# Regrouped early transposes, a split last K tile and a later store of a small vector in a diffusion-transformer block

## The chip, the cores and the metric

The kernel runs on one core of one Trainium2 chip. The metric is device time in microseconds (us) of one execution. A ratio between two kernels is taken over the fast runs of one job, with its 95% interval; it is not quite the ratio of the medians quoted beside it. The jobs ran on different chips, so times are compared within a job.

TensorE multiplies matrices, VectorE (DVE) and ScalarE (ACT) work elementwise, GpSimd (POOL) helps, and SyncE (SP) issues most DMA transfers. In profile lines "PE" is TensorE, "pk", "pacc", "pm", "pn", "pt" are accumulator tiles, and times count from the first instruction. A transfer is issued when it is handed to the DMA queues and lands when its data has arrived. "The chain" is the work that ended last, followed back through what each step waited for.

## The reference

Two batches of 256 tokens, width D = 1152, which is nine chunks of 128. Token tiles 0, 1 belong to batch 0 and tiles 2, 3 to batch 1.

```python
mod = (silu(c) @ w_mod)          # six vectors: shift_a, scale_a, gate_a, shift_m, scale_m, gate_m
h   = layernorm(x) * (1 + scale_a) + shift_a
q, k, v = split(h @ wqkv)
a   = attention(q, k, v) @ wo
x   = x + gate_a * a
h2  = layernorm(x) * (1 + scale_m) + shift_m
out = x + gate_m * (gelu(h2 @ w_fc1) @ w_fc2)
```

## The kernel before

At the start everything is scarce: x and the weights arrive by DMA, the normalised x (`xn`) is transposed on TensorE chunk by chunk, scaled by `1 + scale_a`, and at once used for K. The `w_scale_a` weights come in four groups; `scale_group(3)` serves chunks 6, 7, 8. I call the landing of that last group "the gate".

```python
KGROUPS = [(0, 2), (2, 4), (4, 6), (6, 9)]     # chunks served by each w_scale_a group
KM1 = 6                                        # K tiles 0..5 run chunk by chunk, 6..8 later as panels

def k_step(k, c0=0, c1=T):                     # chunk k into six K tiles, token columns c0:c1
    for m in range(KM1):
        ...
        nc.tensor.matmul(pk[m][:, c0:c1], w_k[:, k, m*P:(m+1)*P], hT0[:, k, c0:c1], ...)

    # ... cut: tiles 0 to 2, chunks 0 and 1
    recip1(3)
    norm1(3, 0, CUT, "d")
    k_step(0, N, N + P)
    k_step(1, N, N + P)
    pt_3 = transpose_x([2, 3], [0, 1])
    for i, k in enumerate((2, 3)):
        modulate(pt_3, i, k, 0, 0, N, "a")     # "a": on ScalarE, "d": on VectorE
    pt_4 = transpose_x([0, 1], [3])
    ...
    k_step(2, 0, N)
    k_step(3, 0, N)
    # ... cut
    nc.vector.transpose(s_rows[...], sT[...])  # s = silu(c), as rows
    store_by_quadrant(s_dram[...], s_rows, B)  # read back at about 28 us as s_b
    # ... cut
    k_step(4)
    scale_group(3)("d")                        # the gate
    modulated_transpose(6)
    k_step(5)
    modulated_transpose(7)
    k_step(6)
    modulated_transpose(8)
    k_step(7)
    k_step(8)
    # ... cut: evictions of K tiles 0..5, panels 6 and 7
    shift_a = vec_section(sT, w_shift_a, "shift_a")   # the shift section, 36 narrow matmuls
    k_panel(8)
    # then hT = hT0 + shift_a, and Q's matmuls
```

## Time and profile before

| | |
|---|---|
| time, median of 3 runs | 243.78 us (243.46 to 243.98) |
| span of the profiled run | 242.1 us, clock 0.999 |
| gate: last `w_scale_a` group issued, landed | 11.13, 20.16 us |
| shift section starts | 30.73 us |
| Q's first matmul | 33.95 us |

These are lines of the page: busy us and share of the span of each engine, then busy tenths in 40 slices of the span.

```profile
PE 235.7 (97%) x1689; PEld 142.8 (59%) x1698; DVE 93.2 (38%) x207; ACT 70.3 (29%) x140; POOL 31.9 (13%) x48
...
PE   8899999999999999999999999999999999999994
```

TensorE is nearly always busy, so only its waits count. The Trainium skill, "Perfetto Trace Analysis", section on the tensor engine instruction, says that the end of a matmul in the profile is an estimate. The trace fits that: a matmul over 512 columns is drawn 379 ns long, but the next one starts 216 ns after it. I therefore measure a wait as start to start, less the usual spacing.

The chain that ended last, of the kernel before, around the gate (columns: start us, us, what, count):

```profile
11.13 9.03 DMA w_scale_a<-in_w_mod_dram
20.16 0.05 issue
20.21 0.83 PE pm L246 x27
21.04 0.24 PE pt L264 x4
21.28 1.29 PE pk L286 x6
```

The chain passes through the DMA. The last matmul in front of the gate started at 19.51, so the wait is 20.21 - 19.51 - 0.216 = 0.48 us.

The same view of the same kernel around the shift section (L417) and the start of Q (L495):

```profile
28.85 1.94 PE pk L315 x9
30.80 1.27 PE pn L417 x36
32.06 0.32 PE pk L315
...
34.11 1.94 PE pacc L495 x9
```

The nine matmuls of K's last tile (the record of one is missing) follow the section (from 32.00 to 33.95) and hide VectorE's preparation of Q's input.

Two more lines of the kernel before, from the timeline of ScalarE (the scalings for fc1) and from that of TensorE (the first fc1 matmuls, L786). The columns are start us, us, engine, line, operation, tiles and shapes, count.

```profile
94.53 3.06 ACT L671 ACTIVATE hT<-hT,shift_m,scale_m 128x256 bf16<-128x256 bf16 x6 [3.42 <-DMA hT<-xn]
...
97.68 1.07 ACT L671 ACTIVATE hT<-hT,shift_m,scale_m 128x256 bf16<-128x256 bf16 x2
```

### The profile page before, as it was taken

To read this page: it belongs to the slowest core of one execution; us is meant where nothing else is said; L and a number is where in the kernel's file an instruction comes from. 1 tells how busy PE (TensorE), PEld (TensorE's weight loads), DVE (VectorE), ACT (ScalarE), POOL (GpSimd) and SP (SyncE) were. 2 spreads that over 40 slices of the span, in tenths; PEclk is the share of its full clock that TensorE was granted. 3 is DMA by queue.
4 is the path that set the end of the run, shared out by engine and by line. 5 is a ranking of instruction groups with operands and counts; after the bars stand their busy time and mean duration, and the time that the engine had idled before them with its cause. 6 is when DMAs were issued, how large, how long until landed. Compare 5 with 4: busy or idle time off the path is not lost.

```text
span 242.1 us, 4022 instructions
## 1 busy us (share of the span) xinstructions
PE 235.7 (97%) x1689; PEld 142.8 (59%) x1698; DVE 93.2 (38%) x207; ACT 70.3 (29%) x140; POOL 31.9 (13%) x48
## 2 busy tenths in 40 slices
PE   8899999999999999999999999999999999999994
PEld 2585444466666666888844444444566656665673
DVE  3761550574694676720000039998010000000001
ACT  6542250543635174782222233322000000000000
POOL 1021000000310516300000000000233111111111
PEclk9999999999999999999999999999999999999999
DMA  6999999999999998799999999994971000000000
GB/s 223 325 331 342 383 357 225 328 376 274 251 323 357 385 278 218 201 226 328 328 328 258 218 298 329 326 327 120 311 224 33 19 16 16 20 20 27 21 16 16
DMA packets 76989, 54.48 MB, mean 225 GB/s; under 512 B 26011, under 2 KB 72491, under 8 KB 76971
## 3 DMA queue, kind: packets, MB, share of 16 engines
q1 hardware_dynamic: 76240, 53.02, 76.9%
q0 software_dynamic: 704, 1.20, 1.5%
q8 instruction: 13, 0.21, 0.4%
q14 instruction: 5, 0.04, 0.0%
q10 hardware_dynamic: 27, 0.00, 0.0%
HBM read 46.90 MB, written 1.19 MB: 199 GB/s over the span
## 4 chain that ended last, share of the span: by engine, by line
PE 90%; SPq 4%; DMA 4%; issue 0%; DVE 0%; DVEq 0%
PE pacc L850 29%; PE pacc L786 29%; PE pacc L689 7%; PE pacc L568 7%; PE pacc L495 5%; DMA w_scale_a<-in_w_mod_dram 4%; SPq L109 3%; PE pk L315 2%; PE pacc L503 2%; PE pk L286 2%; PE pa L603 1%; PE ps_s L523 1%; PE pn L417 1%; SPq L104 1%; PE pg L451 1%
## 5 line engine op out<-in xcount | busy, mean ns | idle before, releaser
L786 PE MATMUL pacc<-hT,w_f 128*128 128x256 bf16 (+1 forms) x427 | 70.3, 325 | 0.3
L850 PE MATMUL pacc<-w_f,gT 128*128 128x384 bf16 (+2 forms) x468 | 70.5, 314 | 0.0
L850 PEld LDWEIGHTS <-gT 128*128 128x128 bf16 x468 | 44.4, 98 | 26.2
L786 PEld LDWEIGHTS <-w_f 128*128 128x128 bf16 x432 | 42.2, 98 | 27.8 <-issue 0.2
L469 DVE SCALAR_TENSOR_TENSOR late<-w_gate_mT,late 128x1152 bf16<-128x1152 bf16 x18 | 24.4, 1358 | 35.8 <-DMA w_gate_mT<-in_w_mod_dram 35.2
L856 DVE TENSOR_TENSOR tmp<-pacc,gate 128x384 f32<-128x384 f32 (+2 forms) x13 | 6.8, 526 | 63.5 <-PE pacc L850 63.5
L824 ACT ACTIVATE gT<-pacc 128x512 bf16<-128x512 f32 x24 | 14.3, 597 | 32.3 <-PE pacc L786 32.3
L469 DVE SCALAR_TENSOR_TENSOR s_spill<-w_scale_m,s_b 128x1152 bf16<-128x1152 bf16 x12 | 16.3, 1357 | 8.9 <-DMA w_scale_m<-in_w_mod_dram 8.5
L858 POOL TENSOR_TENSOR o_sb<-tmp,x 128x384 bf16<-128x384 f32 (+1 forms) x12 | 11.6, 972 | 48.7 <-DVE tmp L856 48.7
L689 PE MATMUL pacc<-w_o,big 128*128 128x384 bf16 (+2 forms) x117 | 17.9, 314 | 0.0
L568 PE MATMUL pacc<-w_v,hT 128*128 128x384 bf16 x108 | 17.9, 326 | 0.0
L689 PEld LDWEIGHTS <-big 128*128 128x128 bf16 x117 | 11.0, 98 | 6.8 <-ACT big L611 0.2
L568 PEld LDWEIGHTS <-hT 128*128 128x128 bf16 x108 | 10.4, 98 | 7.0 <-issue 0.2
L286 PE MATMUL pk<-big,w_k 128*128 128x128 bf16 (+2 forms) x100 | 13.3, 276 | 0.2
L695 POOL TENSOR_TENSOR x<-tmp,x_sb 128x384 f32<-128x384 f32 (+1 forms) x11 | 9.8, 888 | 17.1 <-DVE tmp L694 9.4
L495 PE MATMUL pacc<-hT,w_q 128*128 128x512 bf16 x53 | 11.8, 379 | 0.1
L324 POOL DMA_DIRECT2D gates_dram<-grow x4 | 2.1, 522 | 69.8 <-DVE grow L810 69.8
L802 ACT ACTIVATE gT<-pacc 128x512 bf16<-128x512 f32 x12 | 6.9, 597 | 10.4 <-PE pacc L786 10.4
L286 PEld LDWEIGHTS <-w_k 128*128 128x128 bf16 x102 | 7.8, 97 | 3.1 <-issue 0.3
L495 PEld LDWEIGHTS <-w_q 128*128 128x128 bf16 x54 | 5.3, 98 | 6.4
L694 DVE TENSOR_TENSOR tmp<-pacc,gate 128x384 f32<-128x384 f32 (+2 forms) x13 | 6.7, 522 | 5.4 <-PE pacc L689 5.2
L169 PE MATMUL pwarm<-zeros 128*128 128x512 bf16 x21 | 7.4, 503 | 1.2 <-DVE eps_t L92 1.2
(99 smaller groups left out, 159.5 us busy)
## 6 DMA issues: line engine op xcount, KB each, us to landing
w_f<-in_w_fc_dram SPq DMA_DIRECT2D x14, 864.0 KB, 10.9
w_f<-in_w_fc_dram SPq DMA_DIRECT2D x2, 2592.0 KB, 10.2
w_f<-in_w_fc_dram SPq DMA_DIRECT2D x2, 1728.0 KB, 13.3
w_shift_a<-in_w_mod_dram SPq DMA_DIRECT2D x3, 864.0 KB, 11.2
w_v<-in_wqkv_dram SPq DMA_DIRECT2D x3, 864.0 KB, 6.0
w_gate_a<-in_w_mod_dram SPq DMA_DIRECT2D x3, 864.0 KB, 9.2
w_o<-in_wo_dram SPq DMA_DIRECT2D x3, 864.0 KB, 6.0
w_shift_m<-in_w_mod_dram SPq DMA_DIRECT2D x3, 864.0 KB, 13.0
```

What stands on the lines that cost most here:

```text
L109: nc.sync.dma_start(w_k[:, k, 0:KM1 * P], wqkv_v[:, k, D:D + KM1 * P])
L169: nc.tensor.matmul(dst[:], zeros[:, 0:P], zeros[:], start=True, stop=True)
L286: nc.tensor.matmul(pk[m][:, c0:c1], w_k[:, k, m * P:(m + 1) * P], hT0[:, k, c0:c1], start=(k == 0 and c0 == 0), stop=(k == KD - 1), skip_g ...
L469: nc.vector.scalar_tensor_tensor(spill, wT[:, j, :], 1.0, s_b[b], op0=ALU.mult, op1=ALU.mult, accum_out=dst(j, b),)
L495: nc.tensor.matmul(pq[m][:], w_q[:, k, m * P:(m + 1) * P], hT[:, k, :], start=(k == 0), stop=(k == KD - 1),)
L568: nc.tensor.matmul(pacc[:], hT[:, k, t * P:(t + 1) * P], w_v[:, k, pnl * PW:(pnl + 1) * PW], start=(k == 0), stop=(k == KD - 1),)
L689: nc.tensor.matmul(pacc[:], aT[:, k, t * P:(t + 1) * P], w_o[:, k, c0:c1], start=(k == ks[0]), stop=(k == ks[-1]),)
L695: (nc.vector if (t, i) in ((1, 2), (3, 3)) else nc.gpsimd).tensor_tensor(x1[:, t, c0:c1], tmp[:], x_sb[:, t, c0:c1], op=ALU.add)
L786: nc.tensor.matmul(dst, w_f1[m // KD][:, k, ml * P:(ml + 1) * P], hT[:, k, c0:c1], start=(k == 0), stop=(k == KD - 1),)
L824: nc.scalar.activation(gT[:, m, :], pacc[:], ACT.Gelu_apprx_tanh)
L850: nc.tensor.matmul(pacc[:], gT[:, kk, t * P:(t + 1) * P], w_f2[j][:, r, c0 - n * PW:c0 - n * PW + cw], start=(kk == 0), stop=(kk == KF - 1),)
L858: (nc.vector if last else nc.gpsimd).tensor_tensor(o_sb[:], tmp[:], x1[:, t, c0:c0 + cw], op=ALU.add)
```

## The change

The intent: keep TensorE from waiting in the first 34 us. Chunks 2, 3 of batch 0 are transposed earlier, into one accumulator bank with tiles 1 and 2, and scaled on VectorE; their K matmuls then fill a 0.54 us wait for tile 3's normalisation. Two of chunk 5's six matmuls go in front of the gate. K's last tile is split around the shift section. The store of s moves from about 16 us to about 25 us. The diff's core (loading loops rewritten without a change of order, and smaller moves of `norm1` and `scale_group(2)`, are cut):

```diff
-    def k_step(k, c0=0, c1=T):
-        for m in range(KM1):
+    def k_step(k, c0=0, c1=T, m0=0, m1=KM1):
+        for m in range(m0, m1):
...
-    def k_panel(m):
-        pk[m] = acc_tile([P, T], "pk")
-        for k in range(KD):
+    def k_panel(m, ka=0, kb=KD):
+        if ka == 0:
+            pk[m] = acc_tile([P, T], "pk")
+        for k in range(ka, kb):
...
-    pt_1 = transpose_x([0, 1], [1])
+    pt_1 = aux_tile([P, 1, 8 * P], "pt", BF16)
+    ... # tile 1 of chunks 0, 1 into slots 0, 1
+    for k in (2, 3):
+        for t in range(TPB):
+            transpose_into(pt_1, 2 * (k - 1) + t, k, t)
...
+    for k in (2, 3):
+        modulate(pt_1, 0, k, 0, 2 * (k - 1) * P, N, "d")
+    k_step(0, N, N + P)
+    k_step(1, N, N + P)
     recip1(3)
     norm1(3, 0, CUT, "d")
-    k_step(0, N, N + P)
-    k_step(1, N, N + P)
-    pt_3 = transpose_x([2, 3], [0, 1])
-    for i, k in enumerate((2, 3)):
-        modulate(pt_3, i, k, 0, 0, N, "a")
+    k_step(2, 0, N)
+    k_step(3, 0, N, 0, 3)
     pt_4 = transpose_x([0, 1], [3])
...
-    nc.vector.transpose(s_rows[...], sT[...])
-    store_by_quadrant(s_dram[...], s_rows, B)
...
     k_step(4)
+    k_step(5, m1=2)
     scale_group(3)("d")
     modulated_transpose(6)
-    k_step(5)
+    k_step(5, m0=2)
     modulated_transpose(7)
     k_step(6)
     modulated_transpose(8)
+    nc.vector.transpose(s_rows[...], sT[...])
+    store_by_quadrant(s_dram[...], s_rows, B)
...
+    k_panel(8, 0, 5)
     shift_a = vec_section(sT, w_shift_a, "shift_a")
-    k_panel(8)
+    k_panel(8, 5)
```

More of the change, by code (lines that the diff above doesn't have):

```diff
@@ L102, with load_scale_group @@
     w_k = wide_tile("w_k")
-    for k0, k1 in KGROUPS:
-        nc.sync.dma_start(
-            w_scale_a[:, :, k0 * P:k1 * P],
-            wmod_v[:, :, S_SCALE_A * D + k0 * P:S_SCALE_A * D + k1 * P],
-        )
+    def load_scale_group(g, eng):
+        c0, c1 = KGROUPS[g][0] * P, KGROUPS[g][1] * P
+        eng.dma_start(w_scale_a[:, :, c0:c1], wmod_v[:, :, S_SCALE_A * D + c0:S_SCALE_A * D + c1])
+    for g, (k0, k1) in enumerate(KGROUPS):
+        load_scale_group(g, nc.sync)
         for k in range(k0, k1):
@@ L346 @@
     stats_aggregate(2)
+    norm1(0, CUT, D, "d")
     scale_group(0)("a")
@@ L350, with transpose_into @@
     warm(1, pwarm)
-    pt_1 = transpose_x([0, 1], [1])
+    pt_1 = aux_tile([P, 1, 8 * P], "pt", BF16)
+    def transpose_into(pt, slot, k, t):
+        nc.tensor.transpose(pt[:, 0, slot * P:(slot + 1) * P], xns[t][:, k * P:(k + 1) * P], ident[:])
     for k in range(2):
-        modulate(pt_1, k, k, 1, 0, P, "d")
+        transpose_into(pt_1, k, k, 1)
+    for k in (2, 3):
+        for t in range(TPB):
+            transpose_into(pt_1, 2 * (k - 1) + t, k, t)
+    for k in range(2):
+        modulate(pt_1, 0, k, 1, k * P, P, "d")
     sqrt1(2)
@@ L363 @@
     stats_piece(3, 2)
-    pt_2 = transpose_x([0, 1], [2])
     for k in range(2):
-        modulate(pt_2, k, k, 2, 0, P, "a")
+        transpose_into(pt_1, 6 + k, k, 2)
+    for k in range(2):
+        modulate(pt_1, 0, k, 2, (6 + k) * P, P, "a")
     scale_group(1)("a")
     sqrt1(3)
+    for k in (2, 3):
+        modulate(pt_1, 0, k, 0, 2 * (k - 1) * P, N, "d")
+    k_step(0, N, N + P)
+    k_step(1, N, N + P)
     recip1(3)
     norm1(3, 0, CUT, "d")
-    k_step(0, N, N + P)
-    k_step(1, N, N + P)
-    pt_3 = transpose_x([2, 3], [0, 1])
-    for i, k in enumerate((2, 3)):
-        modulate(pt_3, i, k, 0, 0, N, "a")
+    k_step(2, 0, N)
+    k_step(3, 0, N, 0, 3)
     pt_4 = transpose_x([0, 1], [3])
@@ L378 @@
         modulate(pt_4, k, k, 3, 0, P, "d")
-    k_step(2, 0, N)
-    k_step(3, 0, N)
-    norm1(0, CUT, D, "d")
+    k_step(3, 0, N, 3, KM1)
     norm1(1, CUT, D, "d")
@@ L387 @@
     norm1(3, CUT, D, "d")
-    nc.vector.transpose(s_rows[:].rearrange("p k c -> p (k c)"), sT[:].rearrange("p k c -> p (k c)"))
-    store_by_quadrant(s_dram[:].rearrange("b (k a r) -> a b k r", a=4, r=32), s_rows, B)
+    add2 = scale_group(2)
     k_step(0, N + P, T)
     k_step(1, N + P, T)
-    scale_group(2)("d")
+    add2("d")
     k_step(2, N, T)
@@ L403 @@
     modulated_transpose(8)
+    nc.vector.transpose(s_rows[:].rearrange("p k c -> p (k c)"), sT[:].rearrange("p k c -> p (k c)"))
+    store_by_quadrant(s_dram[:].rearrange("b (k a r) -> a b k r", a=4, r=32), s_rows, B)
     k_step(7)
```

## The prediction

> **What bounds the kernel now.** TensorE: busy 97% of a 242.1 us span at a granted clock of 0.999 (page, parts 1 and 2), 90% of the chain that ended last. After 20.21 us that chain is TensorE, matmul behind matmul; before it lies one DMA, the last group of `w_scale_a`, issued at 11.13 and landed at 20.16. In the timeline the shift section starts at 30.73 us and the Q projection at 33.95, and no wait of size follows. The change touches only the first 34 us, so it can gain (a) what it does in front of the gate at 20.21 instead of behind it, and (b) what it saves or loses from there to 33.95.
>
> **Spacing.** The Trainium skill, "Perfetto Trace Analysis", tensor engine instruction, says a matmul's end is estimated, so I count starts: 512-column matmuls start 216 ns apart in this trace.
>
> **Before the gate.** Chunks 2, 3 are transposed with tile 1; their matmuls fill the 0.54 us hole at 13.2 (waiting for tile 3's normalisation). About 0.2 us should return as a wait for the chunk-2 scaling, now on VectorE behind ScalarE's add. TensorE gets to the gate some 0.3 us earlier, but the DMA doesn't move, so none of this reaches the end. TensorE was already ready at 19.73, 0.48 us too early.
>
> **Across the gate.** Two chunk-5 matmuls (weights landed at 15.97) now run before the last group's matmuls: 2 x 216 = 0.43 us move from behind the gate into the wait. The four left behind it suffice: VectorE's chunk-6 scaling ends about 21.96, chunk 6's matmuls start about 22.2. Gain: 0.43 us, all on the path.
>
> **K's tail.** The shift section's last third of weights lands at 31.47 and is used at 31.51: in the old order TensorE, 0.43 us earlier, would wait 0.3 us. Putting 5 of 9 matmuls of K's last tile in front removes that (first use about 32.2). But only 4 matmuls, 0.86 us, remain behind the section, where 9 (1.94 us) hid the chain from its end, 32.07: VectorE transpose 0.48, two adds to 33.12, semaphore, about 1.1 us. I expect a new TensorE wait of about 0.3 us before the first Q matmul, on VectorE's `hT`. Q starts about 33.82 instead of 33.95: net gain 0.13 us.
>
> **s store.** Its transpose (0.47 us) was off the path; at about 24.5 it fits before K's evictions (VectorE idle 0.90 us there). The rows land about 32.5 instead of 24.16; the `s_b` broadcasts left the queue only at 28.6 to 33.1, so the DMA queue slips 0.6 us at most. `w_v` has 8 us of slack, `w_gate_a` 4, `w_scale_m`'s panel 2.8: no effect on TensorE.
>
> **Predicted.** 243.78 - 0.13 = 243.65 us; 8 in 10 between 243.15 and 244.0. Faster by over 2%: 0.01; within 2%: 0.985; slower by over 2%: 0.005. All matmuls stay; 2% (4.9 us) is out of reach of the 0.5 us at stake.
>
> **What the profile would show.** Right: TensorE still late-started by `w_scale_a` by 0.4 to 0.7 us although two more matmuls precede it; the section without DMA wait; a 0.2 to 0.35 us wait before the first Q matmul, released by VectorE; Q 0.05 to 0.25 us earlier; later stages of equal length. Wrong: Q earlier by 0.4 us or more, no wait before Q, or new DMA waits at 45 to 75 us.
>
> **What would make it wrong.** The last `w_scale_a` group landing 0.2 us off by chance; VectorE late with chunks 2, 3, so that TensorE misses the gate; the later `s_b` load delaying weights or softmax.

## More of the kernel before

Much later, in the second layer norm, the normalised rows are transposed by DMA into `hT`, scaled, and used by fc1:

```python
def ln2_modulate(b, ks=range(KD)):
    for k in ks:
        h = hT[:, k, b * N:(b + 1) * N]
        if b == 0 and k == KD - 1:
            nc.gpsimd.tensor_scalar(h, h, scale_m[...], shift_m[...], ...)
        elif b == 0 or k % 3 == 2:
            nc.scalar.activation(h, h, ACT.Identity, bias=shift_m[...], scale=scale_m[...])
        else:
            nc.vector.tensor_scalar(h, h, scale_m[...], shift_m[...], ...)
```

```profile
97.88 1.85 PE L786 MATMUL pacc<-hT,w_f 128*128 128x256 bf16 x14
```

The PE line shows no idle time. The starts tell otherwise: the seventh fc1 matmul starts at 98.538, the eighth at 98.806, where 0.109 us is usual. Its input is the scaling that ends at 98.75. That is a wait of 0.16 us, hidden by the drawn end of the seventh at 98.810.

## The result, and the profile after

The changed kernel took 243.98 us (median of 6 runs, 243.62 to 244.3); the kernel before, run beside it, 243.82 (6 runs, 243.46 to 243.98). The ratio is 1.0007, 95% interval 0.9994 to 1.002: the same. The profiled span is 242.1 us, as before.

The chain of the changed kernel around the gate:

```profile
18.61 1.73 PE pk L288 x8
20.33 0.65 PE pm L248 x27
20.99 0.24 PE pt L266 x4
21.23 0.86 PE pk L288 x4
```

There is no DMA in it any more. The eight matmuls are chunk 4's and the two of chunk 5. The last group had landed at 19.11, 7.56 us after its issue, and TensorE reached it only at 20.17.

The times from issue to landing of the four `w_scale_a` loads, the kernel before and then the changed one. Of the kernel before, the largest is the last group's; of the changed one, the second group's (7.63) and the last one's (7.56) both round to it:

```profile
DMA to landing us min/median/max: 6.9/7.4/9.0
```

```profile
DMA to landing us min/median/max: 6.9/7.5/7.6
```

The chain of the changed kernel around the shift section (L432) and the start of Q (L511):

```profile
28.80 2.59 PE pk L318 x12
31.39 1.25 PE pn L432 x36
...
32.66 0.49 DVE shift_a L438
...
33.18 0.49 DVE hT L454 x2
33.67 0.04 issue
33.72 2.32 PE pacc L511 x10
```

Now VectorE stands between the section and Q. The last of the four remaining K matmuls started at 33.198 and Q's first at 33.715: a wait of 0.30 us. Still Q starts 0.24 us earlier than before (33.72 against 33.95). That lead is nearly gone at fc2, which starts at 168.19 against 168.24. The chain of the changed kernel near 98 us shows where:

```profile
94.48 3.06 ACT hT L687 x6
97.53 0.19 ACT rstd L657
97.72 0.99 ACT hT L687 x2
98.71 0.04 issue
98.75 1.25 PE pacc L802 x10
```

ScalarE's scaling holds fc1 back, now by 0.35 us instead of 0.16.

### The profile page after: what moved, and what is told of

It reads as the page before. It is cut to its first block, busy times and chain, and to the rows that moved or that the text cites. A ratio compares the mean times of both kernels' runs of the same rounds, so it can differ in the third digit from the quotient of the medians.

```text
span 242.1 us, 4031 instructions
## 1 busy us (share of the span) xinstructions
PE 235.3 (97%) x1698; PEld 142.7 (59%) x1698; DVE 93.4 (39%) x209; ACT 69.5 (29%) x138; POOL 32.0 (13%) x48
## 3 DMA queue, kind: packets, MB, share of 16 engines
HBM read 46.90 MB, written 1.19 MB: 199 GB/s over the span
## 4 chain that ended last, share of the span: by engine, by line
PE 91%; DMA 3%; ACT 2%; DVE 2%; issue 0%; SPq 0%; DVEq 0%
PE pacc L866 29%; PE pacc L802 29%; PE pacc L584 7%; PE pacc L705 6%; PE pacc L511 5%; PE pk L288 4%; DMA w_scale_a<-in_w_mod_dram 3%; PE pacc L519 2%; PE pk L318 2%; ACT hT L687 2%; PE pa L619 1%; PE ps_s L539 1%; PE pn L432 1%; PE pm L248 1%; PE pt L266 1%; PE pg L467 1%
## 5 line engine op out<-in xcount | busy, mean ns | idle before, releaser
L511 PE MATMUL pacc<-hT,w_q 128*128 128x512 bf16 x54 | 11.8, 379 | 0.1
L511 PEld LDWEIGHTS <-w_q 128*128 128x128 bf16 x54 | 5.3, 98 | 6.7 <-issue 0.4
L523 ACT ACTIVATE big<-pacc 128x512 bf16<-128x512 f32 x9 | 4.8, 608 | 11.5 <-PE pacc L511 8.8
```

The source lines that it names most:

```text
L511: nc.tensor.matmul(pq[m][:], w_q[:, k, m * P:(m + 1) * P], hT[:, k, :], start=(k == 0), stop=(k == KD - 1),)
```

## The experiments

### Two kernels twice, and the store alone

The first question was whether the last group's earlier landing came from the later store (theory S) or from chance (theory L). I profiled both kernels again, unedited, moved only the store in the kernel before, and moved only the store back in the changed one.

> The unchanged kernel, profiled a second time. The first profile had the last w_scale_a group landing 9.03 us after its issue (at 20.16) and TensorE waiting for it, the changed kernel's profile 7.56 us (19.11) and no wait. Theory S (the early s store holds that load up): issue to landing again about 9.0 us, last group landed 20.0 to 20.6. Theory L (chance, or start-up jitter of the loads): anywhere from 7.5 to 9.1 us. Under both: Q's first matmul at 33.8 to 34.3, no TensorE wait before it.

Measured: one run of 244.2 us, span 242.4. The group landed 8.15 us after issue, and TensorE did not wait for it. Q started at 33.70, just before the 33.8 to 34.3 that both theories expected. The shift section waited 0.16 us for its weights (landed 31.22), and fc1 waited 0.72 us. So the 0.48 us wait that my forecast took for the kernel's limit is not there in every execution.

> The changed kernel, profiled a second time. Theory S: last w_scale_a group again about 7.6 us from issue to landing and no TensorE wait for it. Theory L: 7.5 to 9.1 us, so perhaps a wait. Under both, if my tail reading is right: a TensorE wait of 0.30 us (0.25 to 0.35) before the first Q matmul, released by VectorE's hT, in every profile of this kernel. The time from the second half of the hT transposes' issue to their landing, 3.29 us before and 3.47 us after, decides how much of Q's lead survives to 98.8 us; if that is chance, it is another number here.

Measured: 243.88 us, span 242.1. The group landed 8.08 us after issue without a wait. The wait before Q was 0.30 us again. Q started at 33.33, 0.39 us earlier than in the first profile of the same kernel, and fc1 waited 0.77 us; fc2 started at 168.22, as late as before. The chain of this repeat of the changed kernel names the source. (In the first profile the same chain ran through VectorE's statistics instead of the DMA; that transpose had landed at 94.37, 0.11 us before ScalarE began, as in the other profiles.)

```profile
90.50 3.90 DMA hT<-xn
...
94.51 3.06 ACT hT L687 x6
97.57 0.19 ACT rstd L657
97.76 0.99 ACT hT L687 x2
98.75 0.04 issue
98.79 1.25 PE pacc L802 x10
```

> The kernel before with one part of the change alone: the s store behind the last chunk's scaling. Theory S: the last w_scale_a group lands 7.4 to 7.8 us after issue, about 1.0 to 1.4 us earlier; TensorE no longer waits for it (0.48 us in the kernel before) and Q starts 0.3 to 0.45 us earlier, unless the shift weights hold it; ratio about 0.9985. Theory L: no fixed difference, ratio 1.000 within 0.0008.

```diff
 # the kernel before
-    nc.vector.transpose(s_rows[...], sT[...])
-    store_by_quadrant(s_dram[...], s_rows, B)
 ...
     modulated_transpose(8)
+    nc.vector.transpose(s_rows[...], sT[...])
+    store_by_quadrant(s_dram[...], s_rows, B)
```

Measured: 243.63 us, ratio 0.9997 (0.9979 to 1.0015); the group landed after 7.40 us and nobody waited for it; fc1 waited 0.56 us. The landing spoke for S, the time for nothing.

> The changed kernel with the s store back where it was before. Theory S: the last w_scale_a group lands 8.7 to 9.2 us after issue, at 20.1 to 20.7, TensorE waits 0.3 to 0.8 us for it; Q starts 0.2 to 0.6 us later than in the changed kernel; time 0.3 us higher. Theory L: no fixed difference, TensorE reaches the gate at about the time of landing, time as the changed kernel within 0.2 us.

The edit is the reverse of the last diff, in the changed kernel. Measured: 244.06 us in the median of the five fast runs, ratio 1.0008 (0.999 to 1.0026). The sixth run, the profiled one, took 414.79 us at a granted clock of 0.56. I use nothing of it. So this run does not decide between S and L; a later one does.

### Taking away the second gate

The new theory, H: a second gate at about 98.8 us, the DMA transpose of `hT` and ScalarE's scalings behind it, swallows what the front gains. The rival, N: the lead of Q is start-up jitter and there is nothing to swallow. Two of ScalarE's scalings for batch 0 went to VectorE, 0.49 us each on ScalarE.

```diff
-            elif b == 0 or k % 3 == 2:
+            elif (b == 0 and k not in (5, 7)) or (b == 1 and k % 3 == 2):
                 nc.scalar.activation(...)
```

> The kernel before, with two of the nine scalings of the second layer norm's output for batch 0 (chunks 5 and 7) moved from ScalarE to VectorE, 0.49 us each on ScalarE. Five profiles so far keep to one sum: fc2's first matmul = Q's first matmul + 63.93 + (TensorE's waits for that scaling at about 98 us) + 70.20. The waits were 0.16 and 0.72 us in two profiles of this kernel. Theory H (a second gate at 98.8 us, set by the hT transposes' landing and ScalarE, swallows what the front gains): waits 0 to 0.1 us here, so the ratio to before is about 0.9975 to 0.9995. Rival N (the gain is not there at all, Q's lead is start-up jitter): the same small gain here, but none of relief_after over relief_before.

Measured: 243.27 us (5 runs) against 243.56, ratio 0.9983 (0.9968 to 0.9998). fc1 did not wait. Q's first matmul came at 33.33, although this front is the kernel's of before.

> The changed kernel with the same two scalings moved. In the two profiles of the changed kernel the waits were 0.35 and 0.77 us, in the one with the earlier Q the longer. Theory H: waits 0 to 0.1 us, the wait of 0.30 us before Q stays, and the kernel is faster than relief_before by Q's lead, 0.2 to 0.4 us: ratio to before 0.9965 to 0.998. Rival N: as relief_before within 0.1 us.

Measured: 243.20 us, ratio 0.9981 (0.9963 to 0.9998). The chain near 98 us is now TensorE alone:

```profile
91.97 5.38 PE pacc L705 x42
97.36 2.73 PE pacc L802 x25
```

H was half right. The second gate is real, and moving two scalings off ScalarE takes it away in both kernels (a later relieved profile keeps 0.06 us). But relief_after is only 0.07 us below relief_before, as N expected. The five times of each spread over 0.3 and 0.46 us, so the times alone do not exclude H's 0.2 us; the profiles say more. Q stood at 33.27 and 33.33, and measured from the landing of the first `w_scale_a` group only 0.07 us apart (the table below). With the gate gone, the change is worth next to nothing.

### K's last tile cut elsewhere

> The changed kernel with the same cut of K's last tile (two and seven) and no relief. Theory H: the wait before Q is gone, Q 0.3 us earlier (33.0 to 33.4), but TensorE's waits at 98 us grow by the same 0.3 us (to 0.65 to 1.1 us) and the time stays that of the changed kernel. Rival N: time falls by 0.3 us, waits at 98 us unchanged.

```diff
-    k_panel(8, 0, 5)
+    k_panel(8, 0, 2)
     shift_a = vec_section(sT, w_shift_a, "shift_a")
-    k_panel(8, 5)
+    k_panel(8, 2)
```

The timeline of this kernel on TensorE:

```profile
29.32 0.81 PE L318 MATMUL pk<-big,w_k 128*128 128x512 bf16 x3
30.06 1.29 PE L432 MATMUL pn<-w_shift_a,sT 128*32 128x288 bf16 x36
31.28 1.68 PE L318 MATMUL pk<-big,w_k 128*128 128x512 bf16 x7
32.80 1.03 PE L511 MATMUL pacc<-hT,w_q 128*128 128x512 bf16 x4
```

Seven matmuls starting at 31.28 reach 31.28 + 7 x 0.216 = 32.79, and Q starts at 32.80: the wait is gone. The time was 243.56 us, ratio 1.0 (0.9983 to 1.0016), and fc1's wait was 0.88 us, as H expected. Q came earlier than expected (33.0 to 33.4), because the loads landed early. That the earlier Q made the wait longer is not shown by this one profile.

> As relief_after, but two matmuls of K's last tile before the shift section and seven behind it, instead of five and four. Seven take 1.51 us, more than the 1.17 us from the section's end to the first Q matmul's data. I expect the 0.30 us wait before Q gone, no wait for the shift weights (landed 30.6 to 30.7 in the changed kernel's profiles, their last third used about 31.1 to 31.5), Q 0.3 us earlier than in relief_after, and the time lower by 0.3 us if nothing gates later: ratio to before 0.995 to 0.9968.

This kernel has both edits above. Measured: 243.04 us, ratio 0.9976 (0.9959 to 0.9992); no wait before Q, none at fc1. It is the fastest version, 0.52 us below after_tail2 in the same job. Against relief_after it gained 0.16 us and not the expected 0.3, and the ratio missed its range (0.995 to 0.9968); in the profiles Q, measured from the first group's landing, did come 0.29 us earlier.

### What is left of the terms in front of the gate

> relief_after with the s store back at its old, early place. From issue to landing the last w_scale_a group took 9.03, 8.15 and 8.18 us in the three fast profiles with the early store and 7.40 to 8.08 us in the six with the late one. Theory S (the early store holds it up): 8.1 to 9.1 us here, the group lands 0.4 to 1.0 us later than in relief_after (18.99) and TensorE, ready at about 19.7, waits 0 to 0.5 us; shift weights also later (30.7 to 31.5). Theory L (chance): 7.4 to 8.1 us. Time: relief_after (243.2) plus 0 to 0.4 us under S, equal within 0.15 under L.

Measured: 243.53 us, ratio 0.9989 (0.9976 to 1.0002). This is its landing line, the largest of the four being the second group's (4.41 to 12.17):

```profile
DMA to landing us min/median/max: 6.8/7.5/7.8
```

The last group took 7.57 us with the early store, as little as with the late one. S as I stated it (8.1 to 9.1 us) fails, and Q kept its distance from the first group. But the shift weights landed at 31.38, as S expected, and the time was 0.33 us above relief_after's in another job, which decides nothing. With the early store the last group took 7.57 to 9.03 us, with the late one 7.35 to 8.08. Three of the four early values lie above all nine late ones, so a smaller effect of the store is neither shown nor excluded, and what made the first profile's 9.03 us stays open.

> relief_after with all six chunk-5 matmuls behind the last w_scale_a group, as in the kernel before. My forecast valued the two moved matmuls at 0.43 us. If TensorE finds that group landed (18.9 to 19.3 in most profiles) it gets there at about 19.3 and starts at once or waits up to 0.1 us; the two matmuls just change places: Q within 0.1 us of relief_after measured from the landing of the first w_scale_a group (24.63), time equal within 0.15 us. If the gate does bind (landing near 20), Q is up to 0.43 us later.

```diff
-    k_step(5, m1=2)
     scale_group(3)("d")
     modulated_transpose(6)
-    k_step(5, m0=2)
+    k_step(5)
```

Measured: 243.43 us, ratio 0.9992 (0.9978 to 1.0005). The chain of this kernel at the gate:

```profile
18.82 1.03 PE pk L288 x4
19.85 0.65 PE pm L248 x27
20.50 0.24 PE pt L266 x4
20.75 1.29 PE pk L288 x6
```

TensorE came to the gate two matmuls earlier, at 19.68, found the group landed (19.16) and did the two matmuls behind it. Q started 24.63 us after the landing of the first `w_scale_a` group, as in relief_after (24.62). The two moved matmuls are worth 0.00 us here. This run also shows the front alone: TensorE reached the gate 10.65 us after group 1's landing, against 11.02 in the profiles of the kernel before in which nothing was late.

### The second gate from the DMA's side

> The changed kernel with one fc1 weight panel (864 KB, 2.7 us of the DMA stream) queued behind the two hT transposes of batch 0 instead of in front of them; ScalarE keeps all its scalings. If the second gate is the hT transposes waiting in the DMA stream behind weights: the first transpose lands 3 to 4 us after issue instead of 4.9 to 6.7, the second 2 to 3.5 us after its own and at 92.5 to 93.8 instead of 94.4; ScalarE starts 0.6 to 1.9 us earlier, TensorE's waits at 98 us are 0 to 0.2 us and the time is 243.2 to 243.4, unless the panel then comes late (used at about 100.6). If the transposes are slow by themselves: landing about 94.4 as before and waits 0.35 to 0.9 us.

```diff
     load_f1(0, 0)
-    load_f1(0, 1)
...
     ln2_transpose(1)
+    load_f1(0, 1)
     load_f1(0, 2)
```

Measured: 243.48 us, ratio 0.9991 (0.9977 to 1.0005). The first transpose took 4.62 us and the second 3.27; the second landed at 94.20 and fc1 waited 0.14 us. The expectation was half met: the wait was short, but the first transpose took longer than the 3 to 4 us expected and the second landed later than 92.5 to 93.8, because it was issued only at 90.94. The interval includes 1, so this order of loads is no clear gain. Nor is the short flight shown to be its doing: two profiles with the old order, before and relief_after_k5_0, have flights nearly as short (4.87 and 3.29 us, 5.02 and 3.31).

> The best kernel so far (ratio 0.9976, interval 0.9959 to 0.9992) once more in a later job, to see whether it holds. All profiles so far keep to: fc2 = Q + 63.93 + waits at 98 us + 70.20, and Q = landing of the first w_scale_a group + 24.63 in the changed kernel, 0.30 less with this cut of K's tail when that landing governs. I expect no wait before Q, no wait at 98 us, Q at 24.3 to 24.7 us after that landing, time 242.9 to 243.4 us, ratio 0.996 to 0.9985.

Measured: 243.13 us against 243.50, ratio 0.9986 (0.9972 to 1.0). The ratio lies just outside the expected 0.996 to 0.9985, and its interval reaches 1: the measured gain is smaller than in the first job, though the intervals overlap. There was again no wait before Q and none at fc1.

### The profiles side by side

All thirteen fast profiles, worked out from their traces. The times are in us from the first instruction. "Group 1" is the first `w_scale_a` group, "group 4" the last; W is what fc1's first matmuls wait in sum.

| profile | group 1 landed | group 4, issue to landing | Q's first start | Q minus group 1 | 2nd `hT` transpose landed | W | fc2's first start |
|---|---|---|---|---|---|---|---|
| before | 8.70 | 9.03 | 33.95 | 25.25 | 94.42 | 0.16 | 168.24 |
| before_rep | 8.84 | 8.15 | 33.70 | 24.86 | 94.73 | 0.72 | 168.55 |
| relief_before | 8.64 | 8.18 | 33.33 | 24.69 | 94.14 | 0.00 | 167.46 |
| store_late_only | 8.60 | 7.40 | 33.49 | 24.89 | 94.36 | 0.56 | 168.18 |
| after | 9.09 | 7.56 | 33.72 | 24.63 | 94.37 | 0.35 | 168.19 |
| after_rep | 8.70 | 8.08 | 33.33 | 24.63 | 94.41 | 0.77 | 168.22 |
| relief_after | 8.64 | 7.89 | 33.27 | 24.62 | 94.26 | 0.00 | 167.40 |
| relief_after_store_early | 9.09 | 7.57 | 33.71 | 24.62 | 94.96 | 0.06 | 167.90 |
| relief_after_k5_0 | 9.03 | 7.66 | 33.66 | 24.63 | 94.14 | 0.00 | 167.79 |
| after_f1_later | 9.14 | 7.35 | 33.76 | 24.62 | 94.20 | 0.14 | 168.02 |
| after_tail2 | 8.14 | 7.77 | 32.80 | 24.65 | 93.99 | 0.88 | 167.81 |
| relief_after_tail2 | 8.81 | 7.65 | 33.14 | 24.33 | 94.02 | 0.00 | 167.27 |
| relief_after_tail2_rep | 9.14 | 7.90 | 33.46 | 24.32 | 94.22 | 0.00 | 167.60 |

Three things can be read from it.

First, fc2's start is Q's start + 63.93 + W + 70.20 in every row, to 0.01 us, and the rest of the kernel takes 73.86 to 73.88 us. So no other difference between these kernels shows in the last 208 us.

Second, with the changed front and the five-and-four cut, Q follows group 1 by 24.62 to 24.63 us in all six profiles. With the front of before it takes 24.69 to 25.25. When nothing else is late the change saves only 0.06 us (24.69 against 24.63), and it guards against late DMAs: the 0.48 us at the gate and 0.05 us for the shift weights in the first profile, and the 0.16 us for the shift weights in the second. In store_late_only group 2 landed 3.33 us behind group 1 instead of 3.1, and that delay also came through. The cut at two saves 0.30 us more (24.33). In after_tail2 both x's second half (6.24 us, group 1 at 8.14) and group 2 (3.60 us behind group 1) came unusually late relative to group 1, and TensorE lost time to both, so Q does not follow group 1 there.

Third, in the seven profiles in which ScalarE does all the scalings, fc2 starts 73.81 to 73.82 us after the second transpose's landing (94.42 + 73.82 = 168.24; 94.73 + 73.82 = 168.55; 93.99 + 73.82 = 167.81). There the landing sets the end. The transpose is issued 57.18 us after Q's start in every profile, and in these seven W is its flight, the time from issue to landing, less 3.13 us (to 0.01 us). So a lead of Q is lost only if the flight grows by as much. That it grows because Q is early is not shown: in all thirteen it varied from 3.27 to 4.07 us, and at nearly the same Q (33.72 and 33.71) it took 3.47 and 4.07. A spread of 0.8 us covers the leads of 0.06 to 0.62 us in the column "Q minus group 1".

The spread has a visible companion. In each run a transfer of 16 KB on the queue that the profile calls "instruction" begins at 88.99 to 89.87 us, inside the first transpose. The Trainium skill, "Runtime: NRT & Kernel Launch", section Terms, says that each engine's instruction memory is refilled in 16 KiB blocks, and "DMA: Bandwidth & Descriptors", section "Issuing engines are not separate DMA queues", that DMAs started by ScalarE, SyncE or GpSimd run on the same 16 DMA engines and interleave; it does not speak of refills there. The traces agree with the size: the packets on this queue (q8) have 16,384 bytes, 13 of them in each profile. The line of the DMA view from 88.5 to 91.5 us, the kernel before and then the changed kernel's repeat (packets, MB, share of 16 engines' time):

```profile
q8 instruction: 1, 0.02, 2.4%
```

```profile
q8 instruction: 1, 0.02, 4.8%
```

The packets themselves took 1.17 and 2.33 us, which are these shares of 16 x 3 us. The packet took 1.10 to 1.19 us in three profiles (before, relief_after_k5_0, after_f1_later), and there the first transpose took 4.62 to 5.02 us and the second 3.27 to 3.31. In the other ten it took 2.33 to 2.55 us, and the transposes 6.12 to 6.70 and 3.47 to 4.07. They go together in all thirteen, and the other twelve packets of each profile took 0.88 to 1.60 us. In the ten, the second transpose landed 2.44 to 2.55 us after the packet's end. But it also landed 3.35 to 3.41 us after the fc1 weights queued in front of it, so the two could have a common cause. That one causes the other was not tried.

## Why the prediction was right, and where it was not

- **Total.** Forecast 243.65 us, 243.15 to 244.0, no clear change; measured 243.98, no clear change. The range held, near its upper end. The terms below were partly wrong and cancelled, so that the total held is partly luck; and a range of 0.85 us would have held any net effect of this size.
- **"Nothing of this reaches the end" (the front).** Wrong. I read the gate from one profile and took it as fixed: "the DMA doesn't move". It landed 7.35 to 9.03 us after issue, and in twelve of thirteen profiles TensorE came later than the group. So the front's work does count. The gain in front is 0.37 us: the gate's matmuls start 11.08 us after group 1's landing with two matmuls (0.43 us) more in front of them, against 11.02 before. The forecast had this size about right (0.3 us) and struck it out.
- **"Gain: 0.43 us, all on the path" (the two chunk-5 matmuls).** This step failed. It measured 0.00 in relief_after_k5_0, because there was no wait to move them into. By luck the sum survives: the front's 0.37 us, which I had struck out, stands in its place.
- **K's tail.** Right in kind and size for the new wait: 0.30 us before Q, on VectorE, in every profile with that cut, and none with seven matmuls behind the section. What the cut avoids is less sure. The forecast gave the old order a 0.3 us wait for the shift weights, from one profile's landing (31.47). An estimate from the six profiles with the five-and-four cut (the section moved 5 x 0.216 us earlier, against the landing of its weights at 30.22 to 31.38) gives 0 to 0.44 us, below 0.3 in five of them. The uncut tail behind the new front was not run. From group 1 on, the terms are 0.37 - 0.30 = 0.07 us, and 0.06 were measured.
- **The s store.** Right so far as shown: the `s_b` load left the queue 0.43 us later (33.08 against 32.65) and TensorE did not wait for it. Whether the early store delayed the last `w_scale_a` group stays open.
- **"No wait of size follows", "later stages of equal length".** Wrong. fc1 waits 0.14 to 0.88 us for ScalarE's scalings behind the `hT` transposes. Its 0.16 us stood in the first profile, under the drawn end of a matmul; I had used starts only where I expected something. The landing behind this wait sets the end of both kernels, and its spread is larger than the change's 0.06 us.

The change therefore moved the time by nothing measurable for two reasons: most of what it saves in front it pays back before Q, and the rest is below the spread of a later wait that it does not touch.

## What to carry to other kernels

Before you count a wait as a limit, profile the unchanged kernel twice: a wait on a DMA can be 0.48 us in one execution and absent in the next. Look for waits by matmul starts over the whole span, not only where the change is, because the next gate decides how much of an early gain arrives. When a tile's matmuls are split around a small computation, leave enough of them behind it to cover the whole chain from its result to the next consumer: here 1.17 us, which seven matmuls of 0.216 us covered and four did not (by the sum, six would do).

## What the Trainium skill lacked or had wrong

- "Perfetto Trace Analysis" says that a matmul's end is estimated, but not that this hides waits: here an end drawn 0.16 us past the next expected start hid a 0.16 us wait, which only start-to-start times showed.
- No page says how long a 16 KiB instruction refill, which the q8 packet is taken to be, occupies its DMA engine, or that it can meet a kernel's transfers: 1.10 to 1.19 us in three profiles and 2.33 to 2.55 us in ten, with the DMA transpose in flight at the time taking 4.62 to 5.02 or 6.12 to 6.70 us.
- "DMA: Bandwidth & Descriptors" has no latency for a small transpose from SBUF to SBUF: 128 x 1152 bf16 took 3.27 to 4.07 us from issue to landing, issued while another such transpose was still in flight.
- No page gives the run-to-run spread of a load's landing: the same 864 KB load in the same place of the queue took 7.35 to 9.03 us.
